# Loads of five batches moved from SyncE's DMA queue to GpSimd's, with a new order of all operations

## The chip, the core and the metric

The kernel runs on one core of one Trainium2 chip. A core has a matrix engine (TensorE, PE in the profile, its weight loads PEld), a vector engine (VectorE, DVE), an activation engine (ScalarE, ACT), GpSimd (POOL) and SyncE (SP). SP computes nothing: it issues DMAs. POOL can issue DMAs too, and here does little else. The transfers themselves run on 16 DMA engines, which all issuing engines share. The metric is the time of one execution on the device, in microseconds (us).

## The reference, cut to what matters

```python
B, H, S, D = 8, 8, 576, 64
def phi(x, c, s):
    r = np.maximum(x, 0.0)
    return np.concatenate([r * c, r * s], axis=-1)
q_p = phi(q, cos_w, sin_w)                      # cos, sin of pi/2 * pos/S
k_p = phi(k, cos_w, sin_w)
kv = np.einsum('bhsf,bhsd->bhfd', k_p, v)
z = np.sum(k_p, axis=2)
num = np.einsum('bhsf,bhfd->bhsd', q_p, kv)
den = np.einsum('bhsf,bhf->bhs', q_p, z)[..., None] + 1e-06
x = (num / den).transpose(0, 2, 1, 3).reshape(B * S, H * D)   # 4608 x 512
h = x @ w_in                                    # 512 x 2048
g = np.maximum(h, 0.0) ** 2
out = g @ w_out                                 # 2048 x 512
```

Linear attention per batch, then two matrix products over all 4608 rows with a squared relu between them. Inputs and output are float32; the kernel multiplies in bfloat16.

## The kernel before, in words

**Tiling.** Each batch has 576 rows: 512 in four groups of 128 (j = 0 to 3) and a tail of 64, put together with the tails of other batches into a ninth "batch", b = 8. The feature dimension of one head is 128 (cos part and sin part).

**Loads.** One batch b has ten load DMAs (`plan_loads`, L708). `ldk` and `ldq` bring the 512 main rows of k and q, 1 MB each, into one buffer `kq` (pool of one, L332). `ldv b.0` and `b.1` bring the main rows of v, half the heads each, 512 KB, into `vs` (pool of one, so the second waits until the first has been spread). `ldv b.2` is two DMAs of 64 KB for v's tail (`vst`, pool of one). `ldkt b.0`, `b.1`, `ldqt b.0`, `b.1` are 64 KB each, the tails of k and q (`kqt`, pool of two). A load can be issued only when the buffer's former content has been read. The weights w_in and w_out come in eight DMAs on POOL at the start and are turned into bfloat16 on the way.

**Attention of a batch** (`plan_att` L747, `plan_q` L797). `cos b.j` and `sin b.j` compute the features of k and q together from `kq` into `fe` (two buffers, j = 0, 1 and j = 2, 3); `cos b.t`, `sin b.t` those of the tail from `kqt` into `fet` (one buffer, L335). `vs b.i` spreads v into the tile `vext` (name of the resource: `ve`). `kv b` (40 matmuls, accumulator kz) needs all features and all of v; `kvz b` copies its result. From batch 2 on the features of q are transposed by DMA: `qTd b.0`, `b.1` (fe) and `b.2` (fet), issued by SP. `num b.j` multiplies them with kvz, `div b.j` divides by the denominator, and `xTd b.i`, again a DMA transpose on SP, makes the operand of the first product. `num b.4` and `div b.4` do two tails at once.

**The products.** Some batches do the first product plainly (`H b.s.tok half`, 8 matmuls of 256 columns, followed by a relu `...r` and a square `...q`); the others by a scheme that saves one product in eight (`G b.s`: P1 to P7 on PE, `seed`, `u2`, `s5` copies, `c11` to `c22` relus, sums `xs` made on DVE). The second product is `Y b` (P1 to P7 of 16 matmuls each, sums `S1` to `S4` on DVE, copies `c..`, stores `st`), for batch 0 the plain `Y0.a..`, `Y0.b..`. The weights' own sums are `w1s..` and `w2t..` on DVE. PSUM has six banks for these accumulators (pool `x`) and two, one buffer, for `num` and `kz` (pool `n`).

**The order.** Nothing reorders work on the chip: every engine runs its instructions in the order in which the program issues them. That order is the string `ORDER` (L23 on), a list of 1061 words. Each word is one planned operation; a star at its end puts it on ACT where it could run on ACT or DVE. `Plan.run` (L220) goes through the words, gives each operation an engine and each buffer a slot, and keeps a forecast of times, by which slots are chosen; the forecast of DMAs is in the class `Transfers` (L132). The forecast is not used on the chip. DMA operations take their place in the queue of the engine that issues them: one that waits for a buffer holds up everything behind it on that queue.

**Which queue.** `plan_loads(b, eng)` puts a batch's loads on SP or on POOL. Batches 0 and 1 are loaded by hand at the start (`begin` L1312, `loads_of_1` L1433), nearly all on POOL. Batch 2 is on POOL, batches 3 to 7 on SP, between the transposes and the stores of the output, which are always on SP (a few of the last stores on ACT).

Of the kernel before, what the change touches and what calls it, by code (L numbers as in the profile page):

```python
# [32 lines left out]
qT1.2 qTc1.1* ldv2.2 Y0.b8 Y0.b9 qTc1.2* num1.1 Y0.b10 div1.1 ldqt2.1 Y0.a8 H0.3.01q* Y0.a9
ldqt2.0 w1s4 Y0.a10 xT1.1 num1.2 Y0.b11 div1.2 Y0.b12 ldkt3.1 Y0.b13 ldkt3.0 w2t1 Y0.b14 vs2.0*
num1.0 ldqt3.0 xT1.2 Y0.a11 div1.0 xTc1.1* ldqt3.1 ldv2.1 Y0.b15 xTc1.2* Y0.a12 w2t2 Y0.c11*
Y0.a13 xT1.0 num1.3 xTc1.0* Y0.a14 div1.3 Y0.a15 Y0.c10* H1.1.01.0 Y0.c00* Y0.st1 w2t3 Y0.c01*
xT1.3 H1.2.00.0 xTc1.3* Y0.st0 H1.1.01r H1.2.01.0 sin2.0* sin2.1 H1.2.10.0 cos2.2 cos2.0*
H1.1.10.0 cos2.1 H1.2.10r sin2.3* H1.3.00.0 qTd2.0 cos2.3 H1.3.10.0 H1.3.00r* sin2.2 cos2.t*
H1.2.01r H1.0.01.0 vs2.1* H1.3.10r qTd2.1 H1.1.11.0 vs2.2 sin2.t* H1.2.00r H1.0.00.0 H1.0.01r*
w2t4 kv2 ldv3.2 H1.0.00r* H1.1.11r* H1.3.00q H1.0.10.0 H1.1.01q kvz2* ldv3.0 ldk3 num2.1  # L40
H1.0.10r* H1.1.00.0 div2.1 ldq3 H1.1.10r* H1.0.11.0 ldqt4.1 H1.1.00r* H1.3.10q H1.2.11.0
H1.1.10q H1.0.11r* H1.1.00q* H1.1.11q num2.2 H1.3.11.0 div2.2 H1.2.11r* H1.3.01.0 H1.3.11r*
ldkt4.1 vs3.2 H1.3.11q num2.3 ldv4.2 H1.3.01r* Y1.P1 div2.3 H1.3.01q* Y1.S1 xTd2.1 num2.0
Y1.seed vs3.0* Y1.S2 Y1.P2 div2.0 ldv3.1 Y1.P6 Y1.c11 xTd2.0 Y1.S3 num1.4 Y1.u2* sin3.1 Y1.P5
cos3.0* qTd2.2 sin3.0 cos3.1 sin3.3* Y1.P7 sin3.2 qTd3.0 Y1.s5* cos3.2 cos3.3* Y1.S4 H2.1.10.0
qTd3.1 vs3.1 H2.0.11.0 sin3.t* div1.4 H2.1.10r* H2.0.00.0 cos3.t* ldv4.0 H2.1.00.0 H2.0.00r ldk4
xs2.3 H2.0.01.0 ldq4 H2.1.00r* H2.0.11r ldkt5.1 Y1.c22 G2.2.P1 H2.0.01r* kv3 xs2.1 G2.2.seed
xs2.2 xs2.4 H2.1.11.0 kvz3* H2.1.00q num3.0 H2.1.11r* G2.2.P2 div3.0 qTd3.2 H2.1.01.0 vs4.2*
G2.2.c11r* H2.1.11q G2.2.P6 H2.1.01r* ldv5.2 xT1.4 w1s3 num3.1 vs4.0* H2.0.10.0 div3.1 G2.2.u2*
Y1.P3 ldv4.1 H2.1.01q* H2.0.10r ldkt4.0 xTc1.4 H2.1.10q* num3.2 Y1.c12 G2.2.P5 xTd3.0 G2.3.P1  # L50
div3.2 G2.2.s5* G2.2.P7 G2.3.seed G2.3.P5 G2.2.c22r num3.3 G2.3.s5* G2.3.P2 div3.3 G2.3.P6
G2.3.c11r* G2.2.P4 G2.3.u2* G2.3.c11q xTd3.1 G2.2.P3 G2.2.c21r* G2.3.P3 sin4.0 cos4.2* G2.3.P7
cos4.1 ldqt4.0 Y2.P1 sin4.1* G2.3.c22r Y1.st0 cos4.0 sin4.3* G2.3.P4 G2.2.c12r qTd4.0 num3.4
G2.3.c12r G2.3.c21r* Y1.P4 sin4.2 Y2.seed G2.3.c21q* cos4.3 vs4.1 G3.0.P1 qTd4.1 G2.3.c12q*
Y2.P2 G2.3.c22q G3.0.seed xs3.1 Y1.c21* xs3.2 Y2.S1 ldv5.0 cos4.t* G3.0.P2 ldq5 G3.0.P5
G3.0.c11r* G3.0.P6 ldk5 Y2.S2 G3.0.s5* G3.1.P1 Y2.c11* G3.1.P5 sin4.t* G3.0.P3 Y2.S4 Y2.P5
G3.1.s5* ldqt6.1 G3.0.u2* div3.4 Y2.P6 xs3.4 xs3.3 ldqt6.0 G3.0.c12r Y1.st1 G3.0.P7 Y2.u2* kv4
G3.0.c22r G3.1.seed Y2.S3 G3.1.P2 kvz4* G3.0.P4 G3.1.c11r* vs5.0 num4.0 G3.1.P6 G3.0.c21r*
div4.0 ldv5.1 G3.2.P1 G3.1.u2* G3.1.P3 ldqt5.0 G3.1.c11q* G3.1.P7 G3.1.c12r qTd4.2 G3.2.P5
Y2.s5* G3.1.c22r num4.2 Y2.P7 G3.2.s5* vs5.2 ldkt6.1 G3.2.seed div4.2 ldv6.2 cos5.1* sin5.0  # L60
G3.2.P2 num4.1 cos5.2 ldkt5.0 G3.2.P6 G3.1.P4 div4.1 G3.2.u2* ldqt5.1 Y2.P3 G3.1.c21r* sin5.1
sin5.2* xTd4.0 Y2.c22 num4.3 G3.2.c11r* Y2.c12 G3.2.P7 vs5.1* G3.3.P1 G3.2.c22r G3.2.P3 div4.3
G3.3.seed G3.3.P5 cos5.0* G3.2.P4 G3.3.P6 G3.3.s5 xTd4.1 G3.3.P2 cos5.3* Y2.P4 G3.3.c11r qTd5.0
cos5.t* G3.2.c12r sin5.t G3.3.u2* G3.3.P3 G3.3.c11q Y2.c21* G3.3.P7 sin5.3 G3.1.c21q* Y2.st0
Y3.P1 G3.3.c22r qTd5.1 G3.2.c21r* G3.3.c12r G3.3.c22q* G3.1.c12q G3.3.P4 kv5 G3.3.c12q
G3.3.c21r* Y3.seed G3.3.c21q G4.0.P1 ldk6 G3.1.c22q* xs4.1 Y3.P2 ldv6.0 xs4.2 kvz5* xs4.3 Y3.S1
G4.0.seed ldq6 num5.0 Y3.c11* G4.0.P6 ldqt7.1 Y3.S2 G4.0.P2 G4.0.u2* G4.0.P5 G4.0.c11r* G4.1.P1
Y3.S4 G4.0.s5* Y3.P6 G4.1.seed ldkt6.0 xs4.4 div5.0 qTd5.2 G4.0.P3 G4.1.P2 G4.0.c12r G4.0.P7
G4.1.c11r* xTd3.2 num5.2 G4.0.c22r G4.1.P6 vs6.2* G4.1.P5 div5.2 G4.1.u2* G4.2.P1 G4.1.s5*
G4.1.P7 ldkt7.1 num5.3 G4.1.c22r G4.0.P4 Y2.st1 G4.1.P3 div5.3 G4.0.c21r* Y3.P5 vs6.0* G4.1.c11q  # L70
G4.2.seed G4.1.c12r ldv6.1 G4.1.c22q* num5.1 Y3.S3 xTd5.1 G4.2.P6 G4.2.P2 Y3.u2* G4.2.P5 G4.2.u2
G4.2.c11r* G4.1.P4 div5.1 Y3.s5* Y3.P7 cos6.0* sin6.0 xTd5.0 G4.2.s5* cos6.2 G4.3.P1 G4.1.c21r*
Y3.P3 Y3.c22 cos6.t* sin6.1 G4.3.seed cos6.3 cos6.1* G4.3.P6 Y3.c12 G4.3.P2 sin6.2* sin6.3
qTd6.0 Y3.P4 G4.3.c11r G4.3.u2* sin6.t G4.1.c12q* vs6.1 G4.2.P7 qTd6.1 G4.3.P5 G4.2.c22r G4.2.P3
G4.3.s5* G4.3.P7 G4.3.c11q* G4.3.P3 G4.3.c22r ldqt7.0 G5.0.P1 Y3.c21* G4.2.c12r G4.2.P4 ldv7.2
G4.3.c22q* G4.3.P4 G4.3.c12r kv6 xs5.1 ldv7.0 G5.0.seed xs5.2 G4.3.c21r* Y3.st0 xs5.3 G5.0.P2
G4.3.c12q kvz6* G5.0.P5 ldq7 G5.0.c11r* xs5.4 G5.0.P6 ldk7 G4.2.c21r G4.1.c21q* num6.0 Y4.P1
div6.0 G4.3.c21q* G5.0.s5 G5.1.P1 Y4.S1 Y4.seed num6.1 G5.0.P3 G5.1.seed Y4.P2 G5.0.u2* Y4.S2
G5.0.c12r G5.1.P2 div6.1 G5.1.P6 G5.0.P7 G5.1.u2* Y4.S3 G5.1.P5 vs7.0* num6.2 Y4.P6 div6.2
# [52 lines left out]
class Transfers:  # L132
# [5 lines left out]
    def __init__(self, at):  # L138
        self.landed, self.written, self.turned, self.last = at, 0.0, False, 0
        self.out, self.lanes = [], []  # L140
# [9 lines left out]
    def issue(self, start, took, ring, lat, service, n, parts=1):  # L150
        size = abs(n)
        if n > 0 and self.turned:
            service += 0.6
        if not ring:
            end = start + took
# [1394 lines left out]
```

## Time and profile before

| | |
|---|---|
| median of 3 runs | 273.72 us (273.46 to 274.08) |
| the profiled execution | 273.9 us, of it 271.8 in the span from the first to the last instruction |
| granted TensorE clock | 0.998 |
| PE, DVE, ACT, POOL busy | 263.3, 226.7, 187.6, 28.9 us |
| DMA queue of SP (q1) | 38.28 MB, 55.0% of 16 engines' span |
| DMA queue of POOL (q0) | 13.76 MB, 19.1% |
| HBM read, written | 36.70 MB, 9.44 MB |

The span is the profile's own clock for the same execution; the 2.1 us beside it are start and end of the program. Busy times are of instructions; matmuls overlap in a pipeline and their ends are modelled, so that short gaps between them do not show as idle time. Issuing a DMA is not busy time on SP (its rows are named SPq), but it is on POOL. In a row of the timeline the first two numbers are the start and the duration; what stands in brackets is the idle time ahead of it and what ended that. The operation's name is not in the rows: `kq<-in_k_dram` is ldk, `qpT<-fe` qTd b.0 or b.1, `qpTt<-fet` qTd b.2, `xT<-xp` xTd, `vst<-in_v_dram` one half of ldv b.2.

### The profile page before, as it was taken

How to read it: one execution, taken by the hardware profiler on the slowest of the kernel's cores; microseconds unless marked ns; L12 is line 12 of the kernel's file. 1: busy time of each engine (PE TensorE's matmuls, PEld its weight loads, DVE VectorE, ACT ScalarE, POOL GpSimd, SP SyncE). 2: the span in 40 equal slices, each digit the busy share in tenths (PEclk: the TensorE clock that was granted, in tenths of full speed). 3: DMA queues.
4: the chain of work that ended last, by engine and by line, in shares of the span. 5: the costliest groups of instructions: out<-in, count | busy, mean ns of one | idle time of the engine just before them, and what ended most of it. 6: DMA issues, size and time to landing. Idle time of an engine off the chain costs nothing.

```text
span 271.8 us, 6753 instructions
## 1 busy us (share of the span) xinstructions
PE 263.3 (97%) x2787; PEld 224.4 (83%) x2792; DVE 226.7 (83%) x403; ACT 187.6 (69%) x292; POOL 28.9 (11%) x47
## 2 busy tenths in 40 slices
PE   8799999999999999999999999999999999999994
PEld 3568767699778888989888998899888888888883
DVE  3874696998997999799989899989849978789952
ACT  5665695888567997889689968996554534955600
POOL 8924446200000000000000000000000000000000
PEclk9999999999999999999999999999999999999999
DMA  7999999897999999999997999680321021010215
GB/s 219 316 204 268 317 280 306 294 299 204 296 218 268 287 272 265 380 148 225 288 286 184 208 325 300 171 159 11 110 56 61 10 112 57 38 42 0 80 43 191
DMA packets 79006, 53.00 MB, mean 195 GB/s; under 512 B 52064, under 2 KB 74592, under 8 KB 78976
## 3 DMA queue, kind: packets, MB, share of 16 engines
q1 hardware_dynamic: 71344, 38.28, 55.0%
q0 software_dynamic: 7040, 13.76, 19.1%
q10 hardware_dynamic: 592, 0.52, 0.6%
q8 instruction: 22, 0.36, 0.5%
q14 instruction: 8, 0.07, 0.1%
HBM read 36.70 MB, written 9.44 MB: 170 GB/s over the span
## 4 chain that ended last, share of the span: by engine, by line
PE 84%; DMA 6%; DVE 4%; POOL 3%; issue 1%; ACT 0%; SPq 0%; POOLq 0%; ACTq 0%
PE ya L461 17%; PE yb L461 14%; PE hb L461 13%; PE hps L461 10%; PE hc L461 8%; PE ha L461 8%; PE yh L461 5%; DMA w1sb<-in_moe_w_in_dram 5%; PE kz L461 3%; PE num L461 3%; PE yc L461 1%; DVE gs L458 1%; DMA qpTt<-fet 1%; PE tq L622 1%; DVE fe L450 1%
## 5 line engine op out<-in xcount | busy, mean ns | idle before, releaser
L461 PEld LDWEIGHTS <-w1sb 128*128 128x128 bf16 x736 | 70.5, 98 | 10.8 <-issue 1.5
L461 PEld LDWEIGHTS <-gs 128*128 128x128 bf16 x512 | 49.7, 98 | 5.8
L461 PEld LDWEIGHTS <-gT 128*128 128x128 bf16 x448 | 43.1, 98 | 10.3 <-issue 0.5
L442 ACT ACTIVATE gT<-gT 128x1024 bf16<-128x1024 bf16 x38 | 39.6, 1060 | 4.0 <-DVE gT L455 2.0
L461 PE MATMUL hps<-xT,w1sb 128*128 128x256 bf16 x320 | 37.9, 273 | 1.2 <-ACT gT L436 0.8
L450 DVE TENSOR_SCALAR fe<-kq,cols 128x1024 bf16<-128x1024 f32 (+1 forms) x44 | 30.1, 722 | 5.2 <-DMA kq<-in_k_dram 3.5
L461 PEld LDWEIGHTS <-w1s 128*128 128x128 bf16 x312 | 29.8, 98 | 3.3
L461 PE MATMUL ya<-w2sb,gT 128*128 128x256 bf16 x256 | 30.6, 273 | 0.4 <-ACT yb L432 0.4
L461 PE MATMUL hb<-xs,w1sb 128*128 128x256 bf16 x208 | 30.1, 272 | 0.0
L448 ACT ACTIVATE fe<-kq,cols 128x1024 bf16<-128x1024 f32 (+1 forms) x28 | 27.6, 1027 | 2.9 <-DMA kq<-in_k_dram 1.6
L461 PE MATMUL ha<-xT,w1sb 128*128 128x256 bf16 x176 | 26.4, 273 | 0.0
L444 DVE TENSOR_TENSOR gT<-gT 128x1024 bf16<-128x1024 bf16 x34 | 23.0, 687 | 1.6 <-ACT gT L436 1.3
L604 DVE TENSOR_TENSOR xp<-num,den 128x512 bf16<-128x512 f32 (+1 forms) x33 | 22.2, 675 | 1.1
L455 DVE CUSTOM_DVE_ANT_0 gT<-hb,s 128x512 bf16<-128x512 f32 x26 | 17.8, 687 | 3.8 <-PE hb L461 3.7
L436 ACT ACTIVATE gT<-ha 128x512 bf16<-128x512 f32 x23 | 13.8, 600 | 9.5 <-PE ha L461 9.3
L436 ACT ACTIVATE gT<-hps 128x512 bf16<-128x512 f32 x27 | 15.6, 595 | 6.4 <-PE hps L461 6.4
L432 ACT COPY hb<-ha 128x512 f32<-128x512 f32 x26 | 15.2, 586 | 6.4 <-DVE gT L438 3.1
L458 DVE TENSOR_TENSOR gs<-gT 128x2048 bf16<-128x2048 bf16 x16 | 19.5, 1217 | 0.1
L455 DVE CUSTOM_DVE_ANT_0 gT<-hc,u 128x512 bf16<-128x512 f32 x26 | 17.5, 685 | 1.1 <-PE hc L461 0.9
L436 ACT ACTIVATE gT<-hb 128x512 bf16<-128x512 f32 x20 | 11.9, 601 | 6.7 <-PE hb L461 6.6
L461 PE MATMUL hc<-xs,w1s 128*128 128x256 bf16 x104 | 15.6, 272 | 0.0
L461 PE MATMUL hb<-xs,w1s 128*128 128x256 bf16 x104 | 15.6, 272 | 0.0
(111 smaller groups left out, 415.0 us busy)
## 6 DMA issues: line engine op xcount, KB each, us to landing
out_dram<-y SPq DMA_DIRECT2D x16, 512.0 KB, 3.6
vs<-in_v_dram SPq DMA_DIRECT2D x10, 512.0 KB, 4.6
kq<-in_k_dram SPq DMA_DIRECT2D x5, 1024.0 KB, 8.2
kq<-in_q_dram SPq DMA_DIRECT2D x5, 1024.0 KB, 9.9
w1sb<-in_moe_w_in_dram POOLq DMA_DIRECT2D x4, 512.0 KB, 12.0
w2sb<-in_moe_w_out_dram POOLq DMA_DIRECT2D x4, 512.0 KB, 10.7
kq<-in_q_dram POOLq DMA_DIRECT2D x2, 1024.0 KB, 11.5
kq<-in_k_dram POOLq DMA_DIRECT2D x2, 1024.0 KB, 11.7
```

Of the source, the lines that this page charges most:

```text
L432: (nc.scalar.copy if e == "ACT" else nc.vector.tensor_copy)(out=out, in_=in_)
L436: nc.scalar.activation(out=out, in_=in_, func=ACTF.Relu)
L442: nc.scalar.activation(out=out, in_=in_, func=ACTF.Square)
L444: nc.vector.tensor_tensor(out=out, in0=in_, in1=in_, op=ALU.mult)
L448: nc.scalar.activation(out=out, in_=in_, func=ACTF.Relu, scale=col)
L450: nc.vector.tensor_scalar(out=out, in0=in_, scalar1=0.0, scalar2=col, op0=ALU.max, op1=ALU.mult)
L455: nc.vector._custom_dve(dve_ops.TENSOR_ADD_SAT, out=out, in0=in0, in1=in1, s0=BIG, s1=0.0)
L458: nc.vector.tensor_tensor(out=out, in0=in0, in1=in1, op=op)
L461: nc.tensor.matmul(out=out, lhsT=lhsT, rhs=rhs, start=start, stop=stop, skip_group_check=True)
L604: nc.vector.tensor_tensor(out=x, in0=n4[:, :, :, 0:D].rearrange("p b (k l) d -> p b k l d", l=2), in1=r.rearrange("p b (k l) -> p b k l", l=2)
L622: nc.tensor.transpose(t[:, h, :], src, ident[:, :])
```

## The change

Batches 3 to 7 are loaded from POOL as batch 2 is. In the forecast a DMA on POOL gets a rule of its own, the durations of POOL's issues are set to 0.95 (main of v), 1.4 (two tails of v) and 0.7 (one tail of k or q), and `ORDER` is replaced by another list of the same 1061 words, with other choices between ACT and DVE. Everything else stays, among it the transposes and stores on SP and all of the start up to about 16 us.

The code:

```diff
@@ class Transfers
     def __init__(self, at):
+        self.loaded = at
         self.landed, self.written, self.turned, self.last = at, 0.0, False, 0
...
     def issue(self, start, took, ring, lat, service, n, parts=1):
         size = abs(n)
+        if not ring:
+            end = start + took
+            if size <= 256 or parts > 1:
+                return start, end, end + lat + 2.0 * CARE
+            self.loaded = max(end + lat, self.loaded + 1.15 * service)
+            return start, end, self.loaded + 1.8
         if n > 0 and self.turned:
             service += 0.6
-        if not ring:
-            end = start + took
-            self.landed = max(end + lat, self.landed + service)
-            self.turned, self.last = n < 0, n
-            return start, end, self.landed + CARE
@@ plan_loads
-                {eng: (0.6, 0.6, 1.3)[i] if eng == "SP" else (0.95, 0.95, 1.4)[i]},
+                {eng: 0.6 if eng == "SP" else 0.95} if i < 2 else {"POOL": 1.4},
...
-                    {eng: 0.65},
+                    {"POOL": 0.7},
@@ main loop
-                got, ve = plan_loads(b + 1, "POOL" if b == 1 else "SP")
+                got, ve = plan_loads(b + 1, "POOL")
```

(`lat` is 2.3 for tails of v, k and q, 4.7 for ldk and ldq, 3.4 for the main rows of v; `CARE` is 1.0.)

Of the order, the stretch from batch 2's loads to the kv product of batch 3. Before:

```diff
-vs1.1 Y0.b7 ldq2 vs1.2* qT1.3 qT1.0 qTc1.3 ldk2 kv1 qTc1.0 ldkt2.0 H0.1.01q qT1.1 ldkt2.1 kvz1*
-qT1.2 qTc1.1* ldv2.2 Y0.b8 Y0.b9 qTc1.2* num1.1 Y0.b10 div1.1 ldqt2.1 Y0.a8 H0.3.01q* Y0.a9
-ldqt2.0 w1s4 Y0.a10 xT1.1 num1.2 Y0.b11 div1.2 Y0.b12 ldkt3.1 Y0.b13 ldkt3.0 w2t1 Y0.b14 vs2.0*
...
-w2t4 kv2 ldv3.2 H1.0.00r* H1.1.11r* H1.3.00q H1.0.10.0 H1.1.01q kvz2* ldv3.0 ldk3 num2.1
-H1.0.10r* H1.1.00.0 div2.1 ldq3 H1.1.10r* H1.0.11.0 ldqt4.1 H1.1.00r* H1.3.10q H1.2.11.0
...
-ldkt4.1 vs3.2 H1.3.11q num2.3 ldv4.2 H1.3.01r* Y1.P1 div2.3 H1.3.01q* Y1.S1 xTd2.1 num2.0
-Y1.seed vs3.0* Y1.S2 Y1.P2 div2.0 ldv3.1 Y1.P6 Y1.c11 xTd2.0 Y1.S3 num1.4 Y1.u2* sin3.1 Y1.P5
-cos3.0* qTd2.2 sin3.0 cos3.1 sin3.3* Y1.P7 sin3.2 qTd3.0 Y1.s5* cos3.2 cos3.3* Y1.S4 H2.1.10.0
```

After:

```diff
+f0.t0* Y0.a0 Y0.a1 ldv2.0 H0.1.11r H0.1.10q* H0.2.11.0 H0.2.11r* H0.0.11r H0.1.11q f0.t1* Y0.a2
...
+Y0.b4 Y0.b5 H0.2.01r Y0.a4 Y0.a5 Y0.a6 Y0.a7 Y0.b6 sin1.1 ldkt2.0 cos1.2* Y0.b7 vs1.0 sin1.3*
+qT1.3 vs1.1 vs1.2 ldkt3.0 sin1.0* cos1.1* qT1.0 qTc1.0 kv1 kvz1 qTc1.3* qT1.1 Y0.b8 H0.1.01q*
+Y0.a8 qT1.2 qTc1.2 qTc1.1* num1.1 div1.1 H0.3.01q* Y0.b9 Y0.b10 Y0.b11 Y0.b12 num1.2 ldqt3.0
+div1.2 w2t1 ldkt2.1 ldqt2.1 ldqt2.0 cos2.t* xT1.1 xTc1.1* sin2.t Y0.b13 Y0.b14 Y0.b15 Y0.c10*
+Y0.a9 Y0.a10 Y0.c11* num1.0 div1.0 ldq2 xT1.2 xTc1.2* Y0.a11 Y0.a12 w2t2 Y0.a13 num1.3 div1.3
+ldv2.2 w2t3 xT1.0 xTc1.0* ldk2 vs2.0* Y0.a14 Y0.a15 H1.0.00.0 vs2.2 Y0.c01* Y0.c00* H1.0.00r*
+H1.1.01.0 H1.1.01r H1.2.01.0 H1.2.01r xT1.3 xTc1.3* cos2.1 sin2.1 ldv2.1 sin2.0* H1.3.00.0
+cos2.0 H1.3.00r* H1.2.00.0 Y0.st1 H1.0.10.0 cos2.2* sin2.2 cos2.3 vs2.1 H1.2.10.0 H1.1.10.0
...
+H1.1.11q H1.3.11.0 H1.3.11r* H1.3.11q H1.3.01.0 num2.3 div2.3 H1.3.01r* H1.3.01q* Y1.S1 xTd2.1
+Y1.S2 Y1.P1 Y1.seed num2.0 div2.0 ldv3.0 Y1.P2 vs3.0* ldk3 ldv3.2 cos3.0* sin3.1* vs3.2 ldqt3.1
+Y1.c11 Y1.P6 Y1.u2* num1.4 Y1.P5 Y1.S3 sin3.0* xTd2.0 cos3.1 H2.0.11.0 div1.4 sin3.2* H2.1.10.0
+qTd2.2 Y0.st0 cos3.3* ldv3.1 vs3.1* Y1.S4 ldv4.2 G2.2.P1 qTd3.0 H2.1.10r xs2.1 H2.1.00.0
+H2.0.00.0 H2.0.11r xs2.3 H2.0.01.0 ldv4.0 w2t4 xs2.2 ldkt4.0 sin3.t* sin3.3* cos3.2 qTd3.1
```

(`H b.s.tok half.0` is the PE part of an H block.) The words of PE stand in nearly the same order in both lists.

## The prediction

> **What bounds the kernel now.** I read the busy times first, then the same by stage.
>
> ```profile
> span 271.8 us, 6753 instructions
> PE 263.3 (97%) x2787; PEld 224.4 (83%) x2792; DVE 226.7 (83%) x403; ACT 187.6 (69%) x292; POOL 28.9 (11%) x47
> ...
> 64.00:86.00 22.00, 20.69 (x245) 18.04 (x243) 20.62 (x38) 14.73 (x22) 0.00 (x0) 1.00 1.05 251
> 86.00:180.00 94.00, 93.95 (x1072) 84.14 (x1071) 87.69 (x162) 81.62 (x127) 0.00 (x0) 1.00 1.02 254
> 180.00:256.00 76.00, 76.00 (x757) 68.02 (x754) 64.21 (x103) 45.15 (x75) 0.00 (x0) 1.00 0.19 60
> ```
>
> The columns after a stage are its length and the busy times of PE, PEld, DVE, ACT and POOL. PE is full from 86 to 256, DVE is second with 87.69 of 94. Between the start and 256 only 64 to 86 has idle PE worth naming, and there the loss is larger than the table shows, since matmul ends overlap. The kv matmuls of batch 2 begin at 61.03, those of batch 3 at 84.32 (chain of waits), 23.3 us apart. Between them the order puts kv2 itself (1.21), eleven H blocks of 8 matmuls (0.873 each), five Y products of 16 (1.745), four num (0.243), one tail num (0.47) and one G product (0.44): 21.4. So 1.9 us are lost; the start (first 22.5 us wait for the third w1 load) and the last stores hold no load of batches 3 to 7. Gain is thus bounded by about 2.3 us: 1.9 and some 0.4 in gaps of 0.1 to 0.2 after it. What makes the loss:
>
> ```profile
> ACT fet L448 <- DMA qpTt<-fet: 2.2, 1, 2.2
> ...
> 70.89 3.51 SPq L649 DMA_TRANSPOSE xT<-xp  x1
> 74.51 0.52 SPq L512 DMA_DIRECT2D vs<-in_v_dram  x1
> 75.13 2.24 SPq L649 DMA_TRANSPOSE xT<-xp  x1
> 77.46 1.22 SPq L640 DMA_TRANSPOSE qpTt<-fet  x1
> ```
>
> First the waits (total, count, longest), then SP's timeline. Batch 3's tail features need the one fet buffer, which the tail transpose qTd2.2 still reads; SP reaches that only at 77.46, behind loads and transposes, and it lands at 80.6. Main features of batch 3 begin at 74.8, when q has landed (74.63).
>
> **Part 1: 50 issues leave SP.** Batches 3 to 7 have ten each: two k/q of about 0.57 us, two v of 0.52, two v tails of 0.61, four kqt tails of 0.62, so 5.9 per batch, 29 us in all. This is paid beside a full PE and is worth nothing by itself; what it can free is the 1.9 above. In the new order qTd2.2 stands behind xTd2.0 alone, which follows div2.0 (72 to 73): it can issue near 74 and land near 77. ACT's wait of 2.2 goes; next in line are batch 3's main features and DVE.
>
> **Part 2: the same issues on POOL.** POOL's own rows give 0.90 for k/q, 0.76 for v, 0.62 for tails: 7.0 per batch, 35 in all, on an idle engine. Price on others: ten DVE features that ran beside a POOL issue took 769 ns on average, 26 that did not 747, 2.9%. 35 us x 0.93 DVE share x 2.9% = 0.95 us of DVE time at most; I take 0.2, since DVE has 6% to spare (bounds 0 and 0.95).
>
> **Part 3: POOL's queue for batch 2.** Batch 2 was on POOL already, but its q load was third in the planned list and is now behind seven issues: ldv2.0, ldkt2.0, ldkt3.0, ldqt3.0, ldkt2.1, ldqt2.1, ldqt2.0.
>
> ```profile
> 34.18 1.78 POOL L418 DMA_DIRECT2D w2sb<-in_moe_w_out_dram  x2 [1.11 <-DMA kq<-in_k_dram]
> 35.95 0.80 POOL L512 DMA_DIRECT2D vs<-in_v_dram  x1
> 40.60 0.90 POOL L502 DMA_DIRECT2D kq<-in_q_dram  x1 [3.84 <-ACT vextt L432]
> 41.48 0.88 POOL L502 DMA_DIRECT2D kq<-in_k_dram  x1
> 42.36 1.26 POOL L505 DMA_DIRECT2D kqt<-in_k_dram  x2
> 43.61 1.22 POOL L515 DMA_DIRECT2D vst<-in_v_dram  x2
> 46.44 0.62 POOL L505 DMA_DIRECT2D kqt<-in_q_dram  x1 [1.60 <-DMA w2sb<-in_moe_w_out_dram]
> 47.88 0.62 POOL L505 DMA_DIRECT2D kqt<-in_q_dram  x1 [0.82 <-DMA vs<-in_v_dram]
> ```
>
> Each wait on a landing here is for the eighth transfer before: 46.44 for w2 issued at 35.04, 47.88 for v at 35.95. So ldq2 becomes the eighth after that w2 load and issues at 46.4 in place of 40.6; ldv2.2 follows v's landing (47.6), and ldk2 goes out at 49.1 to 50.0. A 1 MB load with nothing ahead landed 6.4 us after its issue (k at 129.24): 56.4 in place of 53.7. From there ACT has three features and a relu (3.75) to 60.2, DVE five features and vs2.1 (3.4 + 0.65) to 60.5; kv2 is due at 61.0. Cost nothing, covered by 0.5 us; if k lands 2 us later still, 1.5.
>
> **Part 4: batch 3.** kq is free at 60.3. ldq3 ends its issue at 61.3 and lands at 67.7; ldv3.0 adds 1.6, ldk3 3.5, the two v tails 0.4, and SP's transpose qTd2.1 takes 1.9 of the same DMA time: 75.1. DVE meets vs3.2 (those v tails) ahead of its other work, so Y1.c11, Y1.S3, cos3.1, div1.4, Y1.S4, H2.1.10r, xs2.1, H2.0.11r, xs2.3, w2t4, xs2.2 and cos3.2 queue behind it, and PE's Y1.P5 waits for Y1.c11. By start distances in DVE's timeline (0.63, 0.60, 1.14, 0.67, 1.04, 1.14, 0.60, 0.33, 0.60, 0.33, 1.14, 0.33, 0.67) they take 9.2: 84.3, where kv3 began before. The planner's new rule lets a tail land 4.3 us after its issue (2.3 + 2.0); on POOL the tails issued behind k and q at 42.36 to 44.22 took 9.7 to 10.9. So the freed SP is worth nothing here: I take 0. Bounds: -1.9 (v tails in by 73.1, kv3 at the 82.4 the PE work allows) and +2.0 (both qT transposes inside the loads, tails at 77).
>
> **Part 5: transposes beside loads.** On SP a transpose stood behind or ahead of a load; now it shares. No transpose ran beside a POOL load before. Nearest rows: SP's four kqt tails of 35.7 to 37.8 beside POOL's w2 and v.
>
> ```profile
> 35.69 1.40 SPq L505 DMA_DIRECT2D kqt<-in_k_dram  x2
> 37.14 1.28 SPq L505 DMA_DIRECT2D kqt<-in_q_dram  x2
> ...
> DMA packets 4444, 1.56 MB, mean 240 GB/s; under 512 B 4328, under 2 KB 4328, under 8 KB 4444
> ```
>
> They landed at 42.6, 44.6, 46.5 and 49.0, 2.1 us apart; tails in one queue land 0.2 apart (53.88, 54.05). From 42 to 49 the two queues moved 786 and 776 packets, one for one. The last line (the DMA view from 56.2 to 62.7, in which SP issued two qT transposes and little else) shows what one is: some 2048 packets of 256 B, 128 per DMA engine, 1.9 us alone. One for one with 1 KB packets (1 MB, 64 per engine, in 3.5 us: 55 ns each) that is up to 7.0, 5.1 more; an xT has half. Behind a load in SP's queue they also waited (landing 3.5 after issue against 1.9). Consumers stand some 8 us of PE work behind (qTd4.0 to num4.0: 8.2), and a transpose starts up to 2 us ahead of the load that the same feature frees. I take 0.1 per batch over five batches, 0.5; bounds 0 and 4.0 (0.8 each).
>
> The Trainium skill (DMA: Bandwidth & Descriptors, Queues, rings and completion order) says each DMA engine goes round-robin over the rows by packet; the packet counts agree. By that alone every qT beside a load would pay its 5.1.
>
> **ACT and DVE**: six sin and one cos feature move to ACT, ten relus to DVE among others; 0 on balance, in the bounds above.
>
> **Sum**: 0 + 0.2 + 0 + 0 + 0.5 = +0.7, span 272.5, profiled execution 273.9 + 0.7 = 274.6. The median of the runs is 0.2 lower: 274.4.
>
> **Rivals.**
> (B) The freed SP wins: kq of batch 2 is free by 59, tails land by 73.1, kv3 comes at 82.4. For it: today's ACT wait has its cause on SP; four kqt tails of batch 3 no longer share with w2. Against: Part 4's FIFO. -1.9 on 273.7 and no later cost: 271.8.
> (C) Transposes starve from batch 4 on, where k and q are issued while the last qT runs and PE has no slack; decided when landing passes 8 us after issue. Three of these late by 1 us, and kv3 late by another 1: +4 on 273.7: 277.7. Against: the DMA share falls to 0.19 after 180, so only batches 4 to 7 can pay.
> (D) POOL's descriptors wait for DVE. DVE's casts and features would hold each load back; POOL's issues beside a busy DVE took the 0.62 to 0.90 of an idle one. If the four issues ahead of a k load were each held by one DVE feature (0.75), k would be 3 us late; batch 3's delay reaches PE, where k is needed at once, later ones go into the 8 us that stand between features and kv: +3 on the median's 273.7: 276.7. The Trainium skill (SBUF — State Buffer, SBUF: two separate sides) describes this trap for GpSimd-issued DMAs; the trace's issue rows do not show it.
>
> **Chances.** Forecast 0.40 (273.2 to 275.6), B 0.30 (271.4 to 273.2), C 0.25 (275.6 to 279), D 0.05. The range 271.7 to 278.4 leaves out the ends of B and C. No change means within 0.2% (0.55 us: 273.2 to 274.3), which is about half of the forecast's case. Faster: B and little more, 0.31; same 0.20; slower 0.49.
>
> **What would show it.** ldq2 waiting on w2sb until 46; ACT's wait for qpTt gone; DVE waiting for vst near 74 ahead of vs3.2; kv3 near 84; qT transposes landing more than 4 us after issue beside loads. Wrong if PE has no idle time in 64 to 86 (B), or gains idle stretches past 100 (C).

## The result, and where the time went

| | before | after |
|---|---|---|
| median of the runs | 273.82 us (273.46 to 274.08, 4 runs) | 310.58 us (309.87 to 315.3, 4 runs) |
| ratio | | 1.1335, 95% interval 1.131 to 1.136 |
| span of the profiled execution | 271.8 us | 308.1 us |
| granted TensorE clock | 0.998 | 0.967 |
| SP's queue (q1) | 38.28 MB | 20.58 MB |
| POOL's queue (q0) | 13.76 MB | 31.46 MB |

The change costs 36.8 us. Here and below, a run over 1.5% above its kernel's lowest is slow and left out of the ratio, and where only one run is then left (e5, e7, e14) no ratio is given. The same views of the profile after as were shown of before: first the page's busy times, then the stages (length, then the busy times of PE, PEld, DVE, ACT and POOL, the granted clock, the DMA share and GB/s).

```profile
span 308.1 us, 6784 instructions
PE 271.6 (88%) x2792; PEld 227.7 (74%) x2792; DVE 228.5 (74%) x406; ACT 191.0 (62%) x289; POOL 65.9 (21%) x97
...
64.00:86.00 22.00, 9.12 (x96) 7.61 (x93) 7.01 (x16) 7.02 (x11) 3.02 (x5) 0.77 0.73 153
86.00:108.00 22.00, 20.57 (x253) 18.25 (x251) 20.24 (x37) 18.14 (x26) 7.50 (x11) 1.00 0.99 225
108.00:128.00 20.00, 15.25 (x143) 12.46 (x140) 13.73 (x25) 12.80 (x19) 3.59 (x6) 0.92 1.16 204
180.00:256.00 76.00, 70.97 (x762) 62.59 (x761) 60.34 (x107) 47.66 (x75) 3.90 (x6) 0.98 0.55 134
```

Of the 36.3 us that the span grew by, 28.0 are idle PE (308.1 - 271.6 against 271.8 - 263.3) and 8.3 are PE's own busy time. The latter goes with the clock column: 0.77 in the stage with the long stall, 0.92 in the next bad one, 1.00 between, so after a stall the matmuls themselves ran slower for a while: from 81 to 83 us the granted clock was 0.50, and the 16 matmuls `hps<-xT,w1sb` behind the stall took 372 ns each on average (272 before). About a third of the loss (11.6 us) falls in 64 to 86, where PE worked 9.12 us and before 20.69; DVE and ACT stand still beside it, so neither of them is the bound there. The waits name the first cause (total, count, longest):

```profile
PE num L463 <- DMA qpT<-fe: 21.3, 5, 12.9
DVE fe L452 <- DMA kq<-in_k_dram: 8.1, 4, 2.9
...
ACT fet L450 <- DMA qpTt<-fet: 0.8, 1, 0.8
```

ACT's wait for qpTt, the one stall of before, went from 2.2 to 0.8. In its place PE waits for qpT, which it never did before. The longest of these waits in PE's, POOL's and SP's timelines:

```profile
60.83 4.18 SPq L642 DMA_TRANSPOSE qpT<-fe  x2
...
62.63 0.90 POOL L504 DMA_DIRECT2D kq<-in_q_dram  x1 [7.77 <-ACT fe L450]
63.53 0.76 POOL L514 DMA_DIRECT2D vs<-in_v_dram  x1
64.28 0.89 POOL L504 DMA_DIRECT2D kq<-in_k_dram  x1
...
80.92 0.62 PE L463 MATMUL num<-kvz,qpT 128*128 128x65 bf16 x8 [12.88 <-DMA qpT<-fe]
```

SP issues qTd2.0 at 60.83 and qTd2.1 at 62.67, as soon as the features are there. The same features free kq, so POOL sends 2.5 MB (ldq3, ldv3.0, ldk3) off at the same moment. num2.2 is due at 68 and starts at 80.92. How long these two transposes took is told by the view of the tile qpT (issue ns as min/median/max; issue to landing in us), first after from 60 to 84, then the same two transposes before, from 56 to 64:

```profile
L642 SPq DMA_TRANSPOSE qpT<-fe x2: 1734/2036/2339, 60.8 to 62.7; - x2
DMA to landing us min/median/max: 4.4/11.3/18.2
```

```profile
L640 SPq DMA_TRANSPOSE qpT<-fe x2: 2047/2222/2396, 56.2 to 58.8; - x2
DMA to landing us min/median/max: 3.9/4.2/4.6
```

Before, SP's queue held the pair and behind it, from 62.41, ldv3.0, ldk3 and ldq3:

```profile
56.23 4.57 SPq L640 DMA_TRANSPOSE qpT<-fe  x2
...
63.02 1.40 SPq L502 DMA_DIRECT2D kq<-in_k_dram  x1
```

The last transpose landed at 62.6 and the loads set out as it did. After, the second transpose took 18.2 us. It goes on like that up to batch 6: qTd3 and qTd4 land 8 to 9 us after their issue, qTd6.1 (180.82 to 196.54) 15.7. The pair of batch 7, with no loads beside it, lands in 4.5 and 5.9.

What the two queues moved from 66 to 80 us, while the second transpose was under way (packets, MB, share of the 16 engines' time):

```profile
q0 software_dynamic: 692, 2.55, 70.7%
q1 hardware_dynamic: 1004, 0.25, 17.5%
```

The transpose's packets of 256 B went between the loads' packets of 4096 B, about three of its own to two of theirs, and the loads' took 70.7% of the time.

### The profile page after: what moved, and what is told of

It is laid out like the page before. It is cut to its first block, busy times and chain, and to the rows that moved or that the text cites. A ratio compares the mean times of both kernels' runs of the same rounds, so it can differ in the third digit from the quotient of the medians.

```text
span 308.1 us, 6784 instructions
## 1 busy us (share of the span) xinstructions
PE 271.6 (88%) x2792; PEld 227.7 (74%) x2792; DVE 228.5 (74%) x406; ACT 191.0 (62%) x289; POOL 65.9 (21%) x97
## 3 DMA queue, kind: packets, MB, share of 16 engines
q0 software_dynamic: 12160, 31.46, 38.9%
q1 hardware_dynamic: 47504, 20.58, 31.1%
## 4 chain that ended last, share of the span: by engine, by line
PE 51%; DMA 34%; DVE 5%; POOL 3%; ACT 3%; issue 2%; DVEq 0%; POOLq 0%; ACTq 0%
DMA qpT<-fe 17%; PE yb L463 10%; PE ya L463 10%; PE hb L463 8%; DMA xT<-xp 6%; PE hps L463 6%; PE ha L463 5%; PE hc L463 5%; DMA w1sb<-in_moe_w_in_dram 4%; DMA kq<-in_q_dram 4%; DMA kq<-in_k_dram 3%; PE yh L463 3%; ACT fe L450 2%; PE num L463 2%; PE kz L463 1%
## 5 line engine op out<-in xcount | busy, mean ns | idle before, releaser
L463 PEld LDWEIGHTS <-gT 128*128 128x128 bf16 x448 | 43.2, 98 | 10.3 <-issue 0.5
L444 ACT ACTIVATE gT<-gT 128x1024 bf16<-128x1024 bf16 x39 | 40.9, 1058 | 3.2 <-DVE gT L457 2.7
L450 ACT ACTIVATE fe<-kq,cols 128x1024 bf16<-128x1024 f32 (+1 forms) x35 | 35.5, 1046 | 8.8 <-DMA kq<-in_k_dram 6.0
L463 PE MATMUL hps<-xT,w1sb 128*128 128x256 bf16 x320 | 39.1, 278 | 1.9 <-ACT gT L438 1.5
L463 PE MATMUL num<-kvz,qpT 128*128 128x65 bf16 x256 | 13.7, 198 | 21.4 <-DMA qpT<-fe 21.3
L452 DVE TENSOR_SCALAR fe<-kq,cols 128x1024 bf16<-128x1024 f32 (+1 forms) x37 | 24.9, 704 | 9.6 <-DMA kq<-in_k_dram 8.1
L463 PEld LDWEIGHTS <-qpT 128*128 128x128 bf16 x256 | 11.8, 100 | 25.2 <-DMA qpT<-fe 22.7
L514 POOL DMA_DIRECT2D vs<-in_v_dram x14 | 10.7, 763 | 76.7 <-ACT vext L434 55.2
L438 ACT ACTIVATE gT<-hps 128x512 bf16<-128x512 f32 x21 | 12.0, 594 | 21.6 <-PE hps L463 21.6
L600 DVE TENSOR_SCALAR den<-num 128x8 f32<-128x8 f32 x36 | 5.8, 161 | 25.5 <-PE num L463 25.3
L438 ACT ACTIVATE gT<-ha 128x512 bf16<-128x512 f32 x21 | 12.6, 598 | 16.4 <-PE ha L463 16.2
```

Source lines behind the costliest of these rows:

```text
L438: nc.scalar.activation(out=out, in_=in_, func=ACTF.Relu)
L444: nc.scalar.activation(out=out, in_=in_, func=ACTF.Square)
L450: nc.scalar.activation(out=out, in_=in_, func=ACTF.Relu, scale=col)
L452: nc.vector.tensor_scalar(out=out, in0=in_, scalar1=0.0, scalar2=col, op0=ALU.max, op1=ALU.mult)
L463: nc.tensor.matmul(out=out, lhsT=lhsT, rhs=rhs, start=start, stop=stop, skip_group_check=True)
L514: eng.dma_start(out=vs[b, i][:, :, :, :], in_=src)
```

## The experiments

Three theories were stated at first. T: the transposes share the DMA engines, packet by packet, with POOL's loads and come late. O: the new order itself is the worse one. W: POOL's queue is held up by buffer waits; with it D: POOL's descriptors wait for DVE. The runs beside which they stand gave 273.6 to 275.7 us (medians) for the kernel before.

**Order and queue taken apart.** e1: the new order, loads of batches 3 to 7 on SP again.

```diff
-                got, ve = plan_loads(b + 1, "POOL")
+                got, ve = plan_loads(b + 1, "POOL" if b == 1 else "SP")
```

> The new order, but the loads of batches 3 to 7 issued by SP again (with the old durations in the forecast); batch 2 stays on POOL. Theory T (DMA transposes of SP share each DMA engine packet by packet with POOL's loads, whose packets are 4 KB, and so land late): no POOL load is left beside a transpose, 272 to 279 us. Rival O (the new order itself is worse, whatever the queue): 300 to 311. Rival W (POOL's queue holds loads up while it waits for buffers): as T, 272 to 279.

Measured: 312.97 us (312.86 to 313.33), ratio 1.141 (1.1353 to 1.1467). Against T as it was put, and nearest to O's 300 to 311: taking POOL away gives nothing back. But this order was made for two queues. In one queue ldq3 (issued at 60.74) stands ahead of qTd2.1, which lands only at 71.15 (10.0 us after its issue), and ldk3 stands behind xTd2.1's wait for div2.3. PE's waits for qpT are 4.1 us in all, so most of the loss here is of another kind. One wait is that which part 4 of the prediction was about:

```profile
DVE vextt L434 <- DMA vst<-in_v_dram: 6.6, 1, 6.6
```

e2: the old order, all loads of batches 3 to 7 on POOL (the whole change but ORDER, with the new forecast and issue times, in the kernel before).

> The old order, but the loads of batches 3 to 7 issued by POOL, with the new forecast. T: transposes run beside loads here too, 290 to 325 us, and PE waits for qpT. O: 273 to 278, since the order is the old one. W: 290 to 325, and the waits are for kq, not for qpT.

Measured: 282.91 us (281.44 to 284.38), ratio 1.031 (1.022 to 1.0401). Between the two forecasts. The transposes come late here too (batch 2's pair lands 9.6 and 10.3 us after its issue, the latest of all 11.9), but PE waits for qpT only 1.6 us: their consumers come later still, in batch 2 because kv2 itself is late. So the order of before bears the second queue, but not for nothing: PE's longest idle stretch, 4.8 us at 60.7, is kv2 waiting for vs2.1, whose load stood behind the tails of batch 3 in POOL's queue. The second queue alone costs 9.0 us, the new order on one queue 39.1 (e1), both together 36.8: the two do not add up.

e3: the old order, only the v, k and q tails on POOL.

```diff
-                {eng: (0.6, 0.6, 1.3)[i] if eng == "SP" else (0.95, 0.95, 1.4)[i]},
+                {eng: 0.6 if eng == "SP" else 0.95} if i < 2 else {"POOL": 1.4},
...
-                    {eng: 0.65},
+                    {"POOL": 0.7},
```

> The old order, and only the tails of v, k and q of batches 3 to 7 (six DMAs of 64 KB per batch) on POOL; the 1 MB and 512 KB loads stay on SP. T: 384 KB are 96 packets of 4 KB, 6 per DMA engine and batch, so a transpose loses about 1 us at most: 272 to 277. Rival D (POOL's descriptors wait for DVE): tails late by 2 to 3 us in every batch, 276 to 282. W: 276 to 282 as POOL waits for vst and kqt in turn.

Measured: 277.84 us (274.77 to 281.49), ratio 1.0083 (1.0039 to 1.0127). 30 of the 50 issues thus leave SP and the kernel is not faster: taking them off gained nothing. The tails are a ninth of the bytes, and cost little. The time is at the lower end of D's and W's range and just above T's, so it does not tell them apart.

**The loads held back.** e4: the changed kernel; POOL reads two elements of the last batch's transposed queries ahead of each k and q load (with ldq3 and ldq7 moved later in the order so that this can be).

```diff
+        if b > 2:
+            for i in range(2):
+                nc.gpsimd.tensor_copy(out=seen[:, i : i + 1], in_=qpT[b - 1, i].tile[:, 0, 0, 0:1])
         eng.dma_start(out=kq[b][:, "kq".index(nm)][:, hs, js], in_=main_of(nm, b)[:, hs, js])
```

> The changed kernel, but POOL reads two elements of the transposed q of the batch before (both halves) ahead of each k and q load, so that these 1 MB loads start only when qTd b.0 and b.1 have landed; ldq3 and ldq7 stand a few words later in the order for that. v loads and tails are not held. T: the 13 us that PE waits for qTd2.1 go, and most of the other waits for qpT: 276 to 292 us. W and D: loads come later still and nothing else changes, 308 to 318.

Measured: 324.51 us (322.86 to 326.17), ratio 1.1826. A miss for every theory; its waits:

```profile
POOL seen L506 <- DMA qpT<-fe: 48.4, 8, 9.2
...
DVE fe L452 <- DMA kq<-in_k_dram: 23.6, 4, 13.0
```

PE's waits for qpT fell from 21.3 to 3.6 us, as T said, but the loads now come later than their features are due. kq is one buffer: load, features, transposes and the next load are a ring, and time taken out of one part of it came back in the next.

**Packets made smaller.** e5: 16 bytes between the 1 KB pieces that a load writes.

```diff
-        kq[b] = buf("kq", [P, 2, H, J, D], F32, "kq")
+        kq[b] = buf("kq", [P, 2, H, J * D + 4], F32, "kq")
...
-            vs[b, i] = buf("y" if b == 1 else "vs", [P, HH, J, D], F32, "vs")
+            vs[b, i] = buf("y" if b == 1 else "vs", [P, HH, J * D + 4 * (b > 1)], F32, "vs")
```

> The changed kernel with 16 bytes between the 1 KB pieces that the k, q and v loads write (so that no four of them can be one 4 KB packet); everything else as changed. If the size of the packets is what makes the transposes late (one packet of theirs per packet of the loads, 4096 B in 164 ns against 1024 B in about 50 ns), qTd2.1 lands about 8 us after its issue instead of 18 and the time falls to 285 to 298. If it is the sharing of the bandwidth, or the order's want of slack alone, or GpSimd's descriptors, nothing changes but a microsecond or two: 308 to 313. If the packets stay 4096 B although the pieces no longer join, the run decides nothing on this.

Measured: 328.14 us (319.79 to 329.71). The packet records still show 4096 B for these loads (6656 of them), so that by its own expectation the run decides nothing on the packets' size. Why even its lowest time is 9 us above the changed kernel's median was not tried.

**The two orders crossed.** Each engine's own order is kept, and the five are merged anew. e6: PE, ACT and DVE in the new order, SP and POOL in the old, loads on SP. e7: PE, ACT and DVE in the old order, SP and POOL in the new, loads on POOL. The diff of both is ORDER alone (and e1's line for e6).

> The changed kernel's order on PE, ACT and DVE, with the order of before on SP and GpSimd and the loads of batches 3 to 7 back on SP. If the new order of the compute engines is what has no slack (k and q are released too late, num of batch 2 stands too early), it stays slow: 300 to 315. If the order of the DMA issues is what makes the time (transposes behind loads in one queue, k and q of batch 3 ahead of the queries' transposes), it falls to 274 to 283. Between these, both have a part.

Measured: 298.79 us (297.41 to 300.91), ratio 1.0863 (1.0746 to 1.0981). No wait of PE for qpT is left; the largest is for num1, 5.5 us up to 57.7.

> The order of before on PE, ACT and DVE, with the changed kernel's order on SP and GpSimd and the loads of batches 3 to 7 on GpSimd. If the new order of the compute engines is the larger part, it comes to 275 to 287, near the old order with its loads on GpSimd (282.9). If the order of the DMA issues on the two queues is the larger part, it comes to 295 to 315.

Measured: 312.99 us (306.5 to 318.97). In the run of 312.99 PE waits for qpT four times, up to 5.6 us, 18.6 in all. Either half of the new order beside the other half of the old one thus costs 23 us and more (298.79 against 275.67 for the kernel before beside it; the lowest time, 306.5, against e2's 282.91), so the crossing does not say which half is the dear one: they were made for each other. What it shows is that PE's waits for qpT can go with the new DMA order and POOL's loads under the old compute order, and can be absent under the new one.

**The disputed cost by itself.** In e8 the stages ran into one another, so that none can be read by itself; e9 does the same with each stage held until the one before has landed.

```diff
+        gate()
+        load(nc.gpsimd, 2, False)
+        turn()
+        gate()
+        load(nc.scalar, 4, False)
+        turn()
```

> Nothing of the reference is computed: only stages, one after the other and twice over, of three transposes of 512 KB on SP alone; of loads of q, half of v and k (2.5 MB) on GpSimd alone; and of both at once with the loads on GpSimd, on GpSimd with gaps of 32 bytes between the 1 KB pieces, on ACT's queue, on SP ahead of the transposes, and on GpSimd while DVE works without a break. Packets shared one for one: the first transpose lands about 4 us after issue alone and 9 to 18 beside the 4 KB packets of GpSimd, and 6 to 9 beside 1 KB packets (gaps, or ACT's queue). Sharing of bandwidth alone: the same 8 to 12 us beside each kind of load. Descriptors held up by DVE: the loads take longer only in the stage with DVE busy.

> Nothing of the reference is computed: eight stages, each held until the one before has landed, and the eight twice over. Three transposes of 512 KB on SP alone; q, half of v and k (2.5 MB) on GpSimd alone; both at once with the loads on GpSimd, on ACT's queue, on SP ahead of the transposes, and on GpSimd with DVE busy; two transposes with the loads on GpSimd at the same moment; the loads on ACT's queue alone. Packets shared one for one: the first transpose lands 4 us after its issue alone, 9 to 16 beside the 4 KB packets of GpSimd, and 5 to 8 beside the 1 KB packets of ACT's queue. Bandwidth shared by bytes: 7 to 10 beside either. Descriptors held up by DVE: the loads land over 2 us later only with DVE busy.

The landing times of the transposes in e9's stages (three in each, issued one behind the other): alone; beside 2.5 MB on POOL; beside the same on ACT's queue; on one queue with the loads, where the first transpose was issued ahead of them and two behind; and beside POOL's loads with DVE busy.

```profile
DMA to landing us min/median/max: 3.8/3.9/4.3
...
DMA to landing us min/median/max: 8.3/8.4/13.2
...
DMA to landing us min/median/max: 6.9/8.5/11.5
...
DMA to landing us min/median/max: 3.8/3.9/11.0
...
DMA to landing us min/median/max: 6.9/7.1/13.9
```

How the packets went in the stage with POOL's loads: from 43.4 to 47 us, then from 51 to 54.

```profile
q1 hardware_dynamic: 2048, 0.52, 63.6%
q0 software_dynamic: 13, 0.05, 12.8%
...
q0 software_dynamic: 234, 0.91, 92.6%
q1 hardware_dynamic: 217, 0.05, 12.5%
```

Four things follow.

First, a transpose beside loads of another queue lands 4.4 us later, the next behind it 9 later.

Second, while both queues have work they take turns by packet: 234 packets of the loads (4096 B, median 184 ns) against 217 of the second transpose (256 B, 18 ns). Beside ACT's loads (1024 B, 46 ns), from 63 to 70 us, it is 1749 against 1796. So T's count by packets holds. A pair of transposes has 256 packets for each DMA engine, the loads have 40 on POOL's queue or 160 on ACT's. The pair therefore lets all of the loads in, by the medians an estimated 7.4 us of their packets either way, and the second transpose lands 8.9 and 7.2 us later than alone. That is why the size of the packets matters little here. By the landing of the first transpose alone (8.3 and 8.5) the forecast of shared bandwidth seemed to hold, but beside POOL it had moved its 2048 packets by 47 us, when the loads had moved 13; it landed at 51.8, and why its completion came so much later no run shows.

Third, in one queue a transpose ahead of the loads lands in 3.8, as if they were not there; the one behind them lands in 11.0. The whole stage takes about as long as beside POOL (16.5 us against 16.6, where transposes alone took 7.9 and loads alone 10.7): the queue does not save time, it chooses who waits.

Fourth, DVE's work does not show: D falls (over both rounds the loads landed 8.2 to 11.9 us after their issue without it, 7.9 to 11.7 with it).

**The bytes taken away.** e10: the changed kernel, each k, q and v main load of batches 3 to 7 cut to one head. e12: the same cut in the kernel before.

```diff
+        hs = slice(0, 1) if b > 2 else hs
         eng.dma_start(out=kq[b][:, "kq".index(nm)][:, hs, js], in_=main_of(nm, b)[:, hs, js])
...
-            src = main_of("v", b)[:, i * HH : (i + 1) * HH]
-            eng.dma_start(out=vs[b, i][:, :, :, :], in_=src)
+            n = 1 if b > 2 else HH
+            src = main_of("v", b)[:, i * HH : i * HH + n]
+            eng.dma_start(out=vs[b, i][:, 0:n, :, :], in_=src)
```

> The changed kernel with the k, q and v loads of batches 3 to 7 cut to one head of eight (of four for v); the other heads keep what batch 2 left in the same buffers, so the attention is not the reference's. Every instruction, queue, order and wait stays; only the bytes beside the transposes are gone. If the bytes of GpSimd's loads beside SP's transposes make the time, it falls to 270 to 278. If the new order has no slack even without them, or GpSimd's issues and waits set it, it stays at 290 to 310. Between these, both have a part.

> The kernel before with the k, q and v loads of batches 3 to 7 cut to one head in the same way (the attention is not the reference's): the control of the run with the changed kernel. If the loads hardly set the old kernel's time, 270 to 274; PE's work alone is 271.

Measured: e10 281.16 us (279.57 to 281.64), ratio 1.0238 (1.0165 to 1.0312); e12 273.15 us (272.08 to 274.58), ratio 0.9961 (0.9929 to 0.9994). e10 is between its two forecasts, near the lower one. Every instruction, queue and wait of the changed kernel is still there; without the bytes 29.4 of its 36.8 us are gone, and the same cut takes 0.8 from the kernel before. Of the 29.4, 18.1 are PE's waits for qpT (21.3 to 3.2) and 5.9 PE's own busy time (271.6 to 265.7). The cut also lets k, q and v themselves land earlier, and it was not made in e1, so how much of the rest is late transposes and how much late loads is not told apart. The stage from 64 to 86 and the wait for qpT in e10:

```profile
64.00:86.00 22.00, 18.66 (x219) 15.92 (x217) 16.76 (x33) 15.55 (x22) 5.27 (x9) 0.92 0.68 113
...
PE num L468 <- DMA qpT<-fe: 3.2, 2, 2.9
```

PE works 18.66 us there in place of 9.12. After 86 e10 has no idle stretch over 0.5 us; its other 7.2 us are lost up to batch 3: kv2 starts at 65.05 (before: 60.87), kv3 26.8 us after it (before: 23.3).

**The second queue with the old order.** e11: the kernel before, its ORDER unchanged, with only the k and q main loads on POOL. e15: the same with e4's two reads.

```diff
-                {eng: 0.6 if eng == "SP" else 0.9},
+                {"POOL": 0.9},
                 lambda e, nm=nm: load_main(nm, b, queue(e)),
```

> The kernel before, its order unchanged, with only the k and q main loads of batches 3 to 7 issued by GpSimd; v and the tails stay on SP. If the loads beside the transposes cost time in any order, 276 to 285, with qpT waits on PE. If the old order has slack enough for the later landings, 272 to 275.

Measured: 294.51 us (292.06 to 304.03), ratio 1.0709 (1.0621 to 1.0797), above the whole forecast. The two transposes of batch 2 and PE's wait:

```profile
L640 SPq DMA_TRANSPOSE qpT<-fe x2: 2635/5291/7947, 56.0 to 58.8; - x2
DMA to landing us min/median/max: 4.7/9.6/14.5
...
PE num L461 <- DMA qpT<-fe: 7.6, 1, 7.6
```

In the very same place of the very same order qTd2.1 lands 14.5 us after its issue; its neighbours in time are ldk3 and ldq3, issued on POOL at 58.37 and 59.26. Mind the issue time as well: SP needs 7.9 us to issue it (2.0 before), and the v and tail loads that stayed on SP stand behind it until 66.92. That may be why moving two loads of ten was dearer than moving all of them (e2); it was not tried apart.

> The run with only k and q of batches 3 to 7 on GpSimd in the old order (294.5), with one thing added: before each of these loads GpSimd reads two elements of the last batch's transposed queries, so that the loads set out only when qTd.0 and qTd.1 have landed, which SP's own queue did by its order. If loads beside transposes are what costs, qTd2.1 lands 4 us after its issue again and the time comes to 273 to 279. If GpSimd's queue, its descriptors or its issue costs are to blame, it stays at 288 to 300.

Measured: 289.04 us (287.51 to 290.85), ratio 1.0548 (1.0476 to 1.062). By its number this falls in the range given to GpSimd's queue and issue costs (288 to 300), not in the other. qTd2.1 lands 6.1 us after its issue and PE's waits for qpT are gone, but only 5 of the 20 us came back. The loads set out 7 us later than before (ldk3 at 70.18, before 63.02), and DVE waits 17 us for kq. These waits, as in e4, point to the late loads rather than to the issues: a wait for the landing is a dear way to get what one queue's order gave, where the loads stood ready behind the transposes and set out as these ended. But the run by itself leaves the other reading open.

**What is left of the new order.** e13: e10 with ldq2 and ldk2 right behind batch 1's last feature. e14: that move alone, with full loads. e17: e1 with each k and q load right behind the last qTd of the batch before.

```diff
-... sin1.0* cos1.1* qT1.0 ... num1.0 div1.0 ldq2 xT1.2 ... xTc1.0* ldk2 vs2.0* ...
+... sin1.0* cos1.1* ldq2 ldk2 qT1.0 ... num1.0 div1.0 xT1.2 ... xTc1.0* vs2.0* ...
```

> The changed kernel with the small loads of e10 (one head of eight for k and q of batches 3 to 7, one of four for v; the attention is not the reference's), and ldq2 and ldk2 issued by GpSimd right behind batch 1's last feature, ahead of the tails that the new order has before them. If the 8 us that e10 still has over the kernel before come from k and q of batch 2 being late (PE idle 2.4 us at 60.0 and 3.1 at 69.9), 272 to 277. If they come from elsewhere in the new order, 279 to 283.

Measured: 286.61 us (285.72 to 287.33), ratio 1.0454 (1.0384 to 1.0525). A miss: 5.5 us slower than e10. k2 lands at 52.3 (e10: 60.65), but now the tails of batch 2 are behind it, and the new order has their features first on ACT and DVE, which wait 8.7 and 4.9 us; PE waits 4.6 us for num1. The place of ldq2 was tied to that order and can't be mended alone.

> The changed kernel with full loads and only that move of ldq2 and ldk2. If the late start of batch 2 adds to what the loads beside the transposes cost, 300 to 307. If it only moves the meeting of loads and transposes to an earlier time, 308 to 313. If batch 2's place in GpSimd's queue was the main cause of the loss, 275 to 285.

Measured: 323.04 us (313.97 to 327.04). No gain either, even by the lowest time; in the run of 327.04 PE waits for qpT 33.7 us. This fits a meeting that only moved.

> The new order with the loads of batches 3 to 7 on SP (312.97), with one thing moved: each k and q main load stands in SP's queue right behind the last transpose of the queries of the batch before it, so that none stands ahead of such a transpose and none behind the wait of an attention transpose. If it is the place of the loads against the transposes that makes the time, in one queue as in two, it falls to 280 to 295. If the new order of the compute engines is what cannot be served, it stays at 303 to 315.

Measured: 301.13 us (298.09 to 303.07), ratio 1.098 (1.0881 to 1.1079). Between the forecasts: 12 of e1's 39 us come back and no wait of PE for qpT is left. Now v is late (ACT waits 15.5 us for vs, DVE 5.2). So the place of the loads against the transposes counts in one queue as well, and is not the whole of what the new order costs there.

**With the compute engines at work.** e16: e9's stages, with PE, ACT and DVE busy or idle and with the loads whole or cut to an eighth.

> Nothing of the reference is computed: five stages, held apart, twice over, each with three transposes of 512 KB on SP: alone with PE, ACT and DVE at work throughout; beside 2.5 MB of loads on GpSimd with those engines idle, and with them at work; beside loads of an eighth (0.4 MB: one head each of q, v and k), idle and at work. If the compute engines' traffic is what stretches the meeting of the two queues in the kernel (20 us for 3.7 MB, where the quiet stages took 16.6 for 4), the second transpose lands 13 us after its issue with the engines idle and 16 to 20 with them at work, and beside the small loads 5 and 8. If it is the meeting itself, the two are within 1 us of each other.

Measured: the second transpose lands 13.2 and 13.1 us after its issue with the engines idle, 12.7 and 12.4 with them at work; beside the small loads 5.8 and 6.6, and 6.4 and 5.2. The means differ by 0.6 and 0.4 us, so work on these engines is not what stretched it to 18.2 in the kernel.

## Why the prediction was wrong

Forecast 274.4 us, range 271.7 to 278.4; measured 310.58. The direction was the likelier one of the chances (slower 0.49), the size was far off.

**The step that failed is part 5**, transposes beside loads, as a term of the sum that was mis-sized: "I take 0.1 per batch over five batches, 0.5; bounds 0 and 4.0". PE alone waited 21.3 us for these transposes, and with the bytes of the loads cut (e10) 29.4 us go. It failed in three places.
- The landing. The price was made by packets, which e9 bears out, but for one transpose, beside loads in packets of 1 KB (55 ns), and 0.1 was taken in its place. POOL's loads go in packets of 4096 B (median 164 ns in this stage), and the features that end last release the second transpose of a pair and q, v and k of the next batch at once, 2.5 MB, and the first transpose is still under way. Alone in a stage that is 8.3 for the first and 13.2 for the second; in the kernel 18.2.
- The cover. "Consumers stand some 8 us of PE work behind" was read off batch 4, where qTd4.0 and num4.0 are 8.2 apart. In batch 2 the new order has num2.2 due 5.4 us after qTd2.1's issue. The forecast checked the cover at one place, and not where it was thinnest.
- What the one queue did. "On SP a transpose stood behind or ahead of a load; now it shares" treated the two as much alike. In batch 2 the old order had the pair ahead of the loads, and the queue kept them apart; e9 (3.8 against 8.3) and e11 (14.5 against 3.9, nothing but the queue of two loads changed) show what that was worth.

The term is not a price of the queue alone. With the old order the second queue costs 9.0 us (e2), since the late transposes are covered there; the new order costs 39.1 even on one queue (e1), with only 4.1 us of PE's waits for qpT. The forecast put 0 for the new order in part 4 and for ACT and DVE, and that failed too; by how much beside the late transposes, no run separates.

**Rival C** had the mechanism, with the wrong price and place. It was decided "when landing passes 8 us after issue", and there it was decided; but it was to begin at batch 4 and cost 4 us. It began at batch 2 with 12.9 us in one wait. The DMA share, used against it, is an average: 0.73 in 64 to 86, the worst stage.

**Part 1** was right that the 29 us of issues are worth nothing by themselves: e3 took most of them off and gained nothing. ACT's wait for qpTt fell to 0.8, as forecast. **Rival B** falls with it: no run with loads off SP was faster than before.

**Part 2**: POOL's busy time rose by 37.0 us (35 forecast). DVE's rose by 1.8, for which no cause was sought; the 0.2 was not tried by itself.

**Part 3** was right in its steps and short in the end: ldq2 issued at 46.55 (46.4 forecast), but k2 landed at 58.52, not 56.4, and kv2 began at 62.93, 2.1 us later than before. The upper bound, 1.5 "if k lands 2 us later still", came nearest; the cover of 0.5 us did not hold.

**Part 4**'s wait, DVE held by the v tails ahead of vs3.2, did not come up in the changed kernel, since num2.2 had stopped DVE until 81.6 already; in e1 it is there with 6.6 us. kv3 began at 100.50, not 84.3. How much the new order costs between kv2 and kv3 without the loads is 3.5 us (e10: 26.8 against 23.3), 3.2 of it PE's wait for qpT, where 0 was taken.

**Rival D**: no run shows it. POOL's issues kept 0.76 to 0.90 us, and DVE's work did not delay the loads of e9.

The rule of the Trainium skill (DMA: Bandwidth & Descriptors, Queues, rings and completion order), by which the prediction worked out 5.1 us for every transpose beside a load, came nearer than the 0.1 taken by row: e9 shows 4.4 for a first transpose and 9 for a second. Its turns by packet agree with e9's counts (234 to 217, 1749 to 1796).

What stays open: why the meeting takes longer in the kernel than in the stages (18.2 against 13.2; the packets of both queues are slower there on average, 265 ns against 211 and 26 against 20, though POOL's median is lower, 164 against 184, so that it is some packets that are held up long). Work on PE, ACT and DVE is not it, by e16; contents of other queues and addresses were not tried. Also open is how the cost of the new order in e1, e6 and e17 divides, and what e10's cut would do on one queue. That the planner's forecast caused the tight order is argued from the code alone: in its new branch a load outside SP's ring changes `self.loaded` and leaves `self.landed`, by which transposes are timed, as it was.

## What to carry to other kernels

One queue is also an order: transfers that are wanted soon and stand ahead of large loads in the same queue are served first for nothing (3.8 us in e9), and moving the loads to another queue "to relieve" the first gives that away. The same order can be wrong: behind the loads a transpose landed after 11.0. Before such a move, add up the bytes that the same event releases on both queues, divide by what the DMA engines moved alone, and hold that landing time against the due time of each consumer, at the place where this is shortest. Where a buffer is single, a later load and a later transpose are one ring, and holding the load back only moves the wait, as e4 and e15 show.

## What the runs showed of the hardware

- Issuing waits too: a transpose that SP issues in 1.4 to 2.5 us alone kept SP for 6.4 us as the second beside loads of another queue (e9) and for 8.9 us behind loads in its own (e9), and for 7.9 us in e11, with everything behind it.
- Two queues with work move about as many packets each, at both sizes tried: 234 packets of 4096 B to 217 of 256 B, 1749 of 1024 B to 1796 of 256 B (e9). A transpose of 2048 packets of 256 B is thus held up by far more bytes than its own.
- The two kinds of transfer nearly add up: 7.9 us of transposes and 10.7 us of loads took 16.6 together, with the loads in 4096 B packets; with 1024 B packets on ACT's queue it was 15.3.
- POOL's loads keep their 4096 B packets when the pieces they write are 1 KB with 16 B between (e5); the same loads go as 1024 B packets from SP and from ACT.
- After a stall of 13 us PE's granted clock was 0.50 for 2 us and 1.00 again from 84 us on; matmuls of 256 columns took 372 ns there, 272 before.
